# Pairs 0 and 1 of a gated-attention and MoE kernel: four tokens to a partition, running sums and v spreading on TensorE, and a new order of steps

## The chip, the cores and the metric

The kernel runs on one core of one Trainium2 chip. The metric is the device time of one execution in microseconds, the median of several runs. A core has five engines that run in parallel, each through its own list of instructions: TensorE (PE, matmuls; PEld is its weight load), VectorE (DVE), ScalarE (ACT), GpSimd (POOL) and SyncE (SP, which here only issues DMA transfers).

## The reference

```python
def _attn_ref(q, k, v, f_logit):                 # B, H, S, D = 4, 8, 768, 48
    f = 1.0 / (1.0 + np.exp(-f_logit))
    state = np.zeros((B, H, D, D))
    for t in range(S):
        state = f[:, :, t, :, None] * state + np.einsum('bhd,bhe->bhde', k[:, :, t], v[:, :, t])
        y[:, :, t] = np.einsum('bhd,bhde->bhe', q[:, :, t], state)

def _moe_ref(x, w_in, w_out):                    # x: 3072 x 384, w_in: 384 x 2048, w_out: 2048 x 384
    h = x @ w_in
    return (h * np.cos(h)) @ w_out
```

A state of 48 x 48 per batch and head decays by a gate per row and takes in one outer product of k and v per token; q reads it. The result, with the heads side by side, goes through two matmuls with h * cos(h) between them.

## The kernel before

**Pairs.** The tokens are cut into 12 pairs of 256 tokens (`PAIRS`), each for one batch and all 8 heads; three pairs in a row belong to a batch and hand on the state. A pair has two chunks of 128 tokens (`g`), and a chunk lies on 64 partitions. Partition p holds tokens 2p and 2p+1 (`e` or `x`, 0 and 1) of every head, so that a DMA moves pieces of 2 x 48 floats, 384 bytes.

**Steps of a pair n.** `f`, `k`, `q`, `v` load. `ex` and `ln` make softplus(-f), the negative logarithm of the gate, in `sp`. `fx`, `fy`, `qa`, `ka` bring the two tokens of a partition to one common point (`qa` and `ka` scale the first token of q and k). `cum` is the running sum over the 64 partitions, a matmul with a triangle of ones (`incl`); `eb` and `ei` are its exponentials with either sign, the decay (`b`) and the growth (`bi`). `qm` and `km` multiply q and k with them. `tq`, `tk` transpose the products on PE (pairs 4 to 11: by DMA), and `qkt` copies them out of PSUM. `sc` makes the scores and `am` masks them. `vb` turns v to bf16 and four `vt` copies lay it out for the next matmul. `ps` makes the outer products, `st` adds the state before, `sz` decays it. `y` (scores times v) and `yi` (q times state) share PSUM banks, and `xe` copies the result to bf16 as x.

**Halves.** Pairs 0 and 1 (`HALVES`) do the front part in two halves of four heads, 0 and 1 behind the point: `ex0.1` is pair 0, heads 4 to 7. The other pairs do it for 8 heads at once.

**MoE of unit m** (256 tokens): `h` (12 matmuls to a step j = 0 to 3, written in two parts, h1.20 and h1.21 being the parts of step 2 of unit 1), `co` the cosine on ACT (a Sin with a shift), `g` the product h * cos(h) on DVE, `o` the second matmul, `ot` the copy and `out` the store. The weights come in four slices each (`w0.j` for w_in, `w1.j` for w_out) through slots of the tile g, and `wc` turns each to bf16: h with step j needs wc0.j.

**The order** is written out by hand: the string `ORDER` lists every step with its engine (T PE, S ACT, V DVE, G POOL, Y SP) and, behind it, the numbers of the slots or PSUM banks that it writes. Each engine runs its own steps in that order; `emit` plays it, and semaphores keep the data dependences. `SLOTS` says how many buffers a tile has. A load into a slot waits until the last reader of its previous content has run, and each load on SP waits for the load eight places before it.

**Zero matmuls.** `zf0` to `zf51` multiply zeros into PSUM; their results are not used. `z...` steps fill constant parts of tiles with zeros.

## Time and profile before

| | |
|---|---|
| three runs | 182.61, 183.1, 181.85 us, median 182.61 |
| profiled execution, first to last instruction (the page gives it no other time) | span 178.2 us |
| busy: PE, DVE, ACT, POOL | 170.5, 136.6, 127.2, 112.9 us |
| matmuls and weight loads | 2475 and 2478 |
| DMA | 34.46 MB, mean 193 GB/s, 67456 of 74394 packets under 512 B |
| granted PE clock over the span | 1.00 |

The span leaves out what lies before the first and after the last instruction, so it is shorter than a run's time. A busy PE is one with a matmul in flight: matmuls overlap, and the ends in the trace are modelled. In the groups, `am<-ps,pmask` means that the instruction writes tile am from ps and pmask.

### The profile page before, as it was taken

To read this page: it belongs to the slowest core of one execution; us is meant where nothing else is said; L and a number is where in the kernel's file an instruction comes from. 1 tells how busy PE (TensorE), PEld (TensorE's weight loads), DVE (VectorE), ACT (ScalarE), POOL (GpSimd) and SP (SyncE) were. 2 spreads that over 40 slices of the span, in tenths; PEclk is the share of its full clock that TensorE was granted. 3 is DMA by queue.
4 is the path that set the end of the run, shared out by engine and by line. 5 is a ranking of instruction groups with operands and counts; after the bars stand their busy time and mean duration, and the time that the engine had idled before them with its cause. 6 is when DMAs were issued, how large, how long until landed. Compare 5 with 4: busy or idle time off the path is not lost.

```text
span 178.2 us, 5848 instructions
## 1 busy us (share of the span) xinstructions
PE 170.5 (96%) x2475; PEld 122.8 (69%) x2478; DVE 136.6 (77%) x206; ACT 127.2 (71%) x179; POOL 112.9 (63%) x145
## 2 busy tenths in 40 slices
PE   7897899999999999999999999999999999999992
PEld 2453559786668866788668886668876767777761
DVE  6479999994896989989999797983938699364640
ACT  3887597887899999888997889949754342365630
POOL 8366889797789998979978599768995000000000
PEclk9999999999999999999999999999999999999999
DMA  5999889999999999978899979995039410020042
GB/s 148 261 261 264 307 221 362 328 359 277 293 258 258 222 241 232 289 166 188 246 198 274 255 198 238 178 287 143 2 59 169 144 48 4 0 88 4 0 177 88
DMA packets 74394, 34.46 MB, mean 193 GB/s; under 512 B 67456, under 2 KB 72832, under 8 KB 74368
## 3 DMA queue, kind: packets, MB, share of 16 engines
q1 hardware_dynamic: 73408, 33.59, 78.9%
q10 hardware_dynamic: 960, 0.49, 0.9%
q8 instruction: 19, 0.31, 0.7%
q14 instruction: 7, 0.06, 0.1%
HBM read 25.17 MB, written 4.72 MB: 168 GB/s over the span
## 4 chain that ended last, share of the span: by engine, by line
PE 84%; DVE 6%; SPq 4%; DMA 3%; issue 1%; ACT 1%; DVEq 0%
PE ps L593 36%; PE ps L577 35%; PE ps L529 5%; SPq L296 4%; PE ps L455 3%; DMA k<-in_k_dram 3%; DVE am L459 2%; PE ps L477 2%; DVE qk L404 1%; PE ps L435 1%; PE ps L374 1%; DVE ps L495 1%; ACT w_in_bf L197 1%; DVE x L197 1%; PE ps L264 0%
## 5 line engine op out<-in xcount | busy, mean ns | idle before, releaser
L559 DVE TENSOR_TENSOR g<-ps,co 128x1024 bf16<-128x1024 f32 x48 | 58.0, 1222 | 20.0 <-ACT co L582 17.1
L582 ACT ACTIVATE co<-ps,halfpi 128x1024 bf16<-128x1024 f32 x48 | 53.0, 1114 | 24.5 <-PE ps L577 21.4
L593 PE MATMUL ps<-w_out_bf,g 128*128 128x384 bf16 x384 | 68.0, 326 | 0.0
L577 PE MATMUL ps<-x,w_in_bf 128*128 128x256 bf16 x576 | 66.9, 273 | 0.4 <-ACT w_in_bf L197 0.3
L577 PEld LDWEIGHTS <-w_in_bf 128*128 128x128 bf16 x576 | 55.5, 98 | 9.0 <-ACT w_in_bf L197 0.5
L593 PEld LDWEIGHTS <-g 128*128 128x128 bf16 x384 | 36.2, 98 | 21.5
L459 DVE TENSOR_TENSOR am<-ps,pmask 128x1024 bf16<-128x1024 f32 x24 | 28.8, 1219 | 4.3 <-PE ps L455 4.0
L197 POOL COPY vt<-vb 64x384 bf16<-64x384 bf16 x40 | 20.6, 516 | 3.1 <-ACT vb L197 1.3
L404 POOL TENSOR_TENSOR qk<-q,b 128x384 bf16<-128x384 f32 x21 | 20.9, 1002 | 2.0 <-DVE q L338 1.3
L404 POOL TENSOR_TENSOR qk<-k,bi 128x384 bf16<-128x384 f32 x20 | 19.9, 1001 | 0.7
L264 PE MATMUL ps<-zero 128*128 128x512 bf16 x49 | 14.8, 426 | 1.5 <-DVE zero L203 1.2
L501 DVE TENSOR_TENSOR sz<-ps,b 64x192 bf16<-64x192 f32 x40 | 14.1, 352 | 2.4 <-PE ps L477 1.6
L351 POOL TENSOR_TENSOR k<-k,f 128x384 f32<-128x384 f32 (+1 forms) x13 | 11.8, 909 | 6.0 <-DMA k<-in_k_dram 3.5
L197 ACT COPY ot<-ps 128x384 f32<-128x384 f32 (+1 forms) x15 | 6.6, 456 | 9.6 <-PE ps L593 5.0
L495 DVE TENSOR_TENSOR ps<-ps,sz 64x192 f32<-64x192 f32 x32 | 11.7, 365 | 1.8 <-PE ps L477 0.8
L329 ACT ACTIVATE f<-f 128x768 f32<-128x768 f32 (+1 forms) x14 | 10.4, 744 | 3.3 <-DMA f<-in_f_logit_dram 2.6
L363 POOL TENSOR_TENSOR sp<-ls 128x384 bf16<-128x384 f32 x10 | 10.1, 1007 | 4.0 <-ACT ls L333 3.8
L341 POOL TENSOR_TENSOR q<-f,q 128x384 f32<-128x384 f32 x10 | 10.0, 998 | 3.9 <-ACT f L344 2.8
L197 POOL CAST vb<-v 128x768 bf16<-128x768 f32 x10 | 8.6, 856 | 1.5 <-DMA v<-in_v_dram 1.5
L455 PEld LDWEIGHTS <-qkt 48*64 48x64 bf16 x384 | 6.2, 106 | 4.5 <-issue 2.4
L455 PE MATMUL ps<-qkt 48*64 48x128 bf16 x384 | 8.8, 220 | 0.5 <-DVE am L459 0.2
L264 PEld LDWEIGHTS <-zero 128*128 128x128 bf16 x52 | 4.8, 105 | 5.7 <-issue 1.9
(64 smaller groups left out, 160.9 us busy)
## 6 DMA issues: line engine op xcount, KB each, us to landing
v<-in_v_dram SPq DMA_DIRECT2D x12, 384.0 KB, 5.6
out_dram<-ot SPq DMA_DIRECT2D x22, 192.0 KB, 3.5
f<-in_f_logit_dram SPq DMA_DIRECT2D x10, 384.0 KB, 6.2
k<-in_k_dram SPq DMA_DIRECT2D x10, 384.0 KB, 6.1
q<-in_q_dram SPq DMA_DIRECT2D x10, 384.0 KB, 5.8
g<-in_moe_w_in_dram SPq DMA_DIRECT2D x4, 768.0 KB, 7.0
g<-in_moe_w_out_dram SPq DMA_DIRECT2D x4, 768.0 KB, 6.9
k<-in_k_dram SPq DMA_DIRECT2D x4, 192.0 KB, 4.7
```

Source lines behind the costliest of these rows:

```text
L197: (nc.scalar.copy if e == "ACT" else eng(e).tensor_copy)(out=o, in_=i)
L264: G.step(f"zf{i}", ("PE",), lambda e, dump=dump: nc.tensor.matmul(dump.ap, lhsT=zero[:, 0:128], rhs=zero, start=True, stop=True), writes=[ ...
L351: eng(e).tensor_mul(out=w.ap[:, :, 0, :], in0=w.ap[:, :, 0, :], in1=t.ap[:, :, 0, :])
L404: G.step(f"{nm}{n}.{u}", ("POOL", "DVE") if cut else ("POOL",), lambda e, u=u, j=j, src=src, dec=dec: eng(e).tensor_mul(out=qkp[u][j].ap[: ...
L455: nc.tensor.matmul(o[64 * h:64 * h + 64, r, 2 * a + g, :].rearrange("p (e n) -> p e n", e=2), lhsT=qkv(u)[s, 1, a, g, h, :], rhs=qkv(u)[s, ...
L459: G.step(f"am{n}.{u}", ("DVE",), lambda e, u=u, sc=sc: nc.vector.tensor_mul(out=am[u].ap.rearrange("p r b n -> p (r b) n"), in0=sc.ap.rear ...
L495: nc.vector.tensor_add(out=view()[s], in0=view()[s], in1=S0.ap[s, :, r, :])
L501: eng(e).tensor_mul(out=new.ap[s, :, r, :].rearrange("p (u a) n -> p u a n", u=2), in0=view()[s].rearrange("p (u a) n -> p u a n", u=2), i ...
L559: nc.vector.tensor_mul(out=o.rearrange("p b (n e) -> p b n e", e=2), in0=ph.ap.rearrange("p (b e n) -> p b n e", e=2, n=64), in1=co.ap.rea ...
L577: nc.tensor.matmul(ph.ap[:, i * T:(i + 1) * T].rearrange("p (g t) -> p g t", t=C), lhsT=w_in_bf[:, kk, f0:f0 + 128], rhs=xa[:, :, kk, :], ...
L582: G.step(f"co{m}.{j}", ("ACT",), lambda e, ph=ph, co=co: nc.scalar.activation(out=co.ap, in_=ph.ap, func=AF.Sin, bias=halfpi), reads=[ph], ...
L593: nc.tensor.matmul(po.ap[:, 0:DM], lhsT=gT.ap[:, j, i * C:(i + 1) * C], rhs=w_out_bf[:, j, :], start=(po.first and j == 4 * s), stop=(po.f ...
```

## The change

Pairs 0 and 1 (`QUADS`) read f, k, q and v with **four tokens to a partition**: partition 2m + a holds tokens 4m to 4m+3 of two heads of each four, the heads alternating between even and odd partitions. DMA pieces are 768 bytes. v is loaded in two halves too.

- `fx`, `qa` and `ka` of these pairs are gone. The running sum is taken for every token: `cum` runs seven wide matmuls (`every`), with triangles that connect only partitions of the same parity (`qincl`, `qstrict`), and the result is 384 wide for half a pair, not 192. `ei` is written over f, `eb` into a new tile `bq`.
- `vb` becomes two passes, each multiplying v by a column of 0 and 1 (`odd`) that keeps the heads of one parity. A new step `vs` spreads v over the partitions with 16 matmuls, and two copies from PSUM (`vt`) replace four copies from SBUF.
- `ps` multiplies pieces of 96 columns instead of 48. Masks, transposes and the gate of units 0 and 1 follow the new order of tokens.
- New constants: `cqi` (four operations on DVE), `cqs` (two) and `cqm` (seven) on POOL.
- `zf` goes from 52 to 15 steps, and the whole `ORDER` is new.

The core of the diff:

```diff
+QUADS = (0, 1)
-ZEROS = 52
+ZEROS = 15
...
         G.step(name, ("SP", "ACT") if name in ("f0.0", "f0.1") else ("SP",), lambda e: eng(e).dma_start(
-            out=val.ap.rearrange("p h e d -> p h (e d)"),
-            in_=tok.rearrange("h (p e) d -> p h (e d)", e=2)), writes=[val])
+            out=val.ap.rearrange("p (r f) e d -> p r (f e d)", f=2) if quad else val.ap.rearrange("p h e d -> p h (e d)"),
+            in_=tok.rearrange("h (m t) d -> m h (t d)", t=4) if quad else
+            tok.rearrange("h (p e) d -> p h (e d)", e=2)), writes=[val])
...
+        sp, bt, bi = Val(spS), Val(bqS if quad else bS), f if quad else Val(biS)
...
+            if quad:
+                continue
             G.step(f"fx{n}{u}", ("ACT",), lambda e, t=t, s=s: gate_of(e, t, s), reads=[s], writes=[te], table="E")
...
+        def every(e, u):
+            w, o = sph[u].ap, pcs[u].ap[:, 0:DM].rearrange("p (j r d) -> p j r d", j=4, r=2)
+            for j in range(4):
+                row = w[:, j, None, :, 0:D]
+                nc.tensor.matmul(o[:, j:4], lhsT=qincl, rhs=row.broadcast_to([128, 4 - j, 2, D]), start=(j == 0), stop=False)
+                if j:
+                    nc.tensor.matmul(o[:, 0:j], lhsT=qstrict, rhs=row.broadcast_to([128, j, 2, D]), start=False, stop=False)
+            for j in range(4):
+                nc.tensor.matmul(pcs[u].ap[:, DM:DM + 4], lhsT=w[:, j].rearrange("p r d -> p (r d)"),
+                                 rhs=qhalf.rearrange("p a g -> p (a g)"), start=False, stop=(j == 3))
...
+                def only(e, a=a):
+                    o, i = vb.ap[:, a].rearrange("p j h d -> p h j d"), byj(vv.ap)
+                    if e == "ACT":
+                        nc.scalar.activation(out=o, in_=i, func=AF.Copy, scale=odd[:, a:a + 1])
+                    else:
+                        eng(e).tensor_scalar_mul(out=o, in0=i, scalar1=odd[:, a:a + 1])
+                G.step(f"vb{n}.{a}", ("POOL", "ACT"), only, reads=[vv, qi_v], writes=[vbp[a]])
...
+            def spread(e):
+                for a in range(2):
+                    for j in range(4):
+                        for g in range(2):
+                            t = slice(64 * g, 64 * g + 64)
+                            rows = pv.ap.rearrange("p (g x) -> p g x", g=2)[32 * j:32 * j + 32, g, 0:DM]
+                            nc.tensor.matmul(rows.rearrange("p (u a n) -> p a u n", u=2, a=2)[:, a], lhsT=qsel[t, a, :],
+                                             rhs=vb.ap[t, a, j].rearrange("p (u r) d -> p u (r d)", u=2),
+                                             start=(a == 0), stop=(a == 1))
+            G.step(f"vs{n}", ("PE",), spread, reads=[vb, qs_v], writes=[pv])
```

**On SP**, the load queue from its first entry. Names carry the slot number: f_0 is slot 0 of f. Shapes of 128x4x96 and 128x2x192 are halves of a pair (0.197 MB). Before, f0.1 stands first, then f1.1, k0.1, the whole v0, q0.1, k0.0 (f0.0 goes over ACT's queue):

```order
L296 DMA f_0_94<-in_f_logit_dram 128x4x96
L296 DMA f_1_95<-in_f_logit_dram 128x4x96
L296 DMA k_0_97<-in_k_dram 128x4x96
L296 DMA v_2_105<-in_v_dram 128x8x96
L296 DMA q_0_100<-in_q_dram 128x4x96
```

Now f0.1, f1.0, k0.1, both halves of v0, k0.0, f1.1, q0.1 and k1.0 come first, then q0.0, k1.1 and both q1. The second piece shows what follows on them: f3, f2 (into the slot of f0), v1, the first two slices of w_in, q3 (into the slot of q0) and k3:

```order
L329 DMA f_1_101<-in_f_logit_dram 128x2x192
L329 DMA f_0_100<-in_f_logit_dram 128x2x192
L329 DMA k_2_105<-in_k_dram 128x2x192
L329 DMA v_0_109<-in_v_dram 128x2x192 x2
L329 DMA k_2_105<-in_k_dram 128x2x192
```

```order
L329 DMA q_1_107<-in_q_dram 128x2x192 x2
L329 DMA f_2_102<-in_f_logit_dram 128x8x96
L329 DMA f_1_101<-in_f_logit_dram 128x8x96
L329 DMA v_1_110<-in_v_dram 128x2x192 x2
L313 DMA g_2_155<-in_moe_w_in_dram 128x3x512
L313 DMA g_4_157<-in_moe_w_in_dram 128x3x512
L329 DMA q_0_106<-in_q_dram 128x8x96
L329 DMA k_0_103<-in_k_dram 128x8x96
```

v0 has moved ahead of q, and f2, which now waits for the last reader of f0, stands ahead of v1 and of the first weights.

**On DVE**, from its first product (km0.1, the first row of each piece) on. Before, the scaling of q (L338) and of k (L351) and products (L404) alternate with the state (L501, L495):

```order
L404 TENSOR_TENSOR qk_118<-k_97,bi_116 128x8x48
L231 MEMSET vt_124 128x16x2x8
L338 SCALAR_TENSOR_TENSOR q_100<-f_94,q_100 128x4x48
L404 TENSOR_TENSOR qk_118<-q_100,b_113 128x8x48
L404 TENSOR_TENSOR qk_118<-k_97,bi_116 128x8x48
L197 COPY qkt_127<-ps_159 128x1024
L231 MEMSET qk_119 128x32x8
L501 TENSOR_TENSOR sz_136<-ps_159,b_113 64x4x48
```

Now there are three products (L459), and the state and the first masked scores (L558) follow:

```order
L459 TENSOR_TENSOR qk_123<-k_105,f_101 128x2x4x48
L260 MEMSET sz_146 128x192
L459 TENSOR_TENSOR qk_123<-k_105,f_101 128x2x4x48
L459 TENSOR_TENSOR qk_123<-q_106,bq_132 128x2x4x48
L609 TENSOR_TENSOR sz_147<-ps_171,bq_132 64x4x48 x2
L603 TENSOR_TENSOR ps_168<-ps_168,sz_147 64x192
L609 TENSOR_TENSOR sz_146<-ps_168,bq_132 64x4x48
L194 COPY qkt_136<-ps_169 128x1024
L558 TENSOR_TENSOR am_141<-ps_171,qmask 128x1024
```

The other five products of the two pairs have moved to **POOL**, whose list from the selection of v0 (L480) to the cast of the first weights reads now:

```order
L480 TENSOR_SCALAR vq_129<-v_109,odd 128x4x4x48 x2
L260 MEMSET vt_135 128x16x2x16
L459 TENSOR_TENSOR qk_123<-q_106,bq_132 128x2x4x48
L459 TENSOR_TENSOR qk_124<-k_104,f_100 128x2x4x48
L459 TENSOR_TENSOR qk_124<-q_107,bq_131 128x2x4x48 x2
L459 TENSOR_TENSOR qk_124<-k_104,f_100 128x2x4x48
L403 TENSOR_TENSOR sp_114<-ls_116 128x8x48
L480 TENSOR_SCALAR vq_130<-v_110,odd 128x4x4x48
L403 TENSOR_TENSOR sp_112<-ls_115 128x8x48
L194 CAST w_in_bf<-g_155 128x3x512
```

and read, from the cast of v0 to the same place, before (L351 scales k, L363 adds the two tokens' sums):

```order
L197 CAST vb_121<-v_105 128x768
L351 TENSOR_TENSOR k_97<-k_97,f_94 128x4x48
L197 COPY vt_124<-vb_121 64x8x48
L231 MEMSET sz_136 128x384
L197 COPY vt_124<-vb_121 64x8x48 x2
L363 TENSOR_TENSOR sp_106<-ls_110 128x8x48
L197 CAST vb_120<-v_104 128x768
L197 COPY vt_123<-vb_120 64x8x48
L404 TENSOR_TENSOR qk_117<-q_101,b_111 128x8x48
L197 COPY vt_123<-vb_120 64x8x48
L351 TENSOR_TENSOR k_99<-k_99,f_95 128x4x48
L363 TENSOR_TENSOR sp_107<-ls_109 128x8x48
```

The copies of v have left POOL, and four products more stand between v and the first weight cast.

293 lines of the change are left out of this document (181 added, 112 removed).

## The prediction

> **What bounds the kernel now.** I read the share of busy time first, then three stretches of the span, then the timeline around the place where they meet.
>
> ```profile
> PE 170.5 (96%) x2475; PEld 122.8 (69%) x2478; DVE 136.6 (77%) x206; ACT 127.2 (71%) x179; POOL 112.9 (63%) x145
> ...
> 0.00:25.19 25.19, 21.20 (x287) 11.06 (x291) 19.27 (x48) 17.91 (x38) 17.51 (x31) 1.00 1.00 241
> 25.19:32.85 7.66, 7.27 (x128) 6.00 (x129) 7.38 (x12) 6.52 (x8) 7.09 (x7) 1.00 1.06 341
> 32.85:174.97 142.12, 142.02 (x2060) 105.69 (x2060) 109.62 (x147) 102.49 (x134) 88.34 (x108) 1.00 0.77 180
> ...
> L264 PE MATMUL ps<-zero 128*128 128x512 bf16 x49 | 14.8, 426 | 1.5 <-DVE zero L203 1.2 <-issue 0.2
> ```
>
> The stretch rows give start and end, length, then busy time of PE, PEld, DVE, ACT and POOL, the granted clock, DMA share and GB/s. From 32.85 us to the last matmul PE is busy 142.02 of 142.12 us: nothing that shortens another engine's work there can shorten the span. Before 25.19 PE looks busy too, but 14.8 us of it is the zero matmuls (their recorded ends overlap), which compute nothing. So the kernel is a **front**, in which PE waits for data, and a **block** of 142.1 us of PE work. The block begins with the third weight slice, h1.20:
>
> ```profile
> 21.85 2.87 POOL L197 CAST w_in_bf<-g 128x1536 bf16<-128x1536 f32 x2
> 25.19 1.47 PE L577 MATMUL ps<-x,w_in_bf 128*128 128x256 bf16 x12
> 31.34 1.46 ACT L197 CAST w_in_bf<-g 128x1536 bf16<-128x1536 f32 x1
> 32.85 4.10 PE L577 MATMUL ps<-x,w_in_bf 128*128 128x256 bf16 x36 [0.30 <-ACT w_in_bf L197]
> ```
>
> Both orders place the same PE steps ahead of h1.20, except that sc3.1 now follows it. **The question is when h1.20 can start.**
>
> **Loads.** Tensors arrive in the order of SP's queue.
>
> ```profile
> 4.00:14.00 10.00, 9.46 (x111) 5.05 (x110) 6.17 (x19) 8.37 (x21) 5.36 (x10) 1.00 1.27 261
> 28.00:30.00 2.00, 2.00 (x20) 1.79 (x19) 1.96 (x4) 1.17 (x2) 1.92 (x3) 1.00 1.03 390
> 7.45 0.82 POOL L197 CAST vb<-v 128x768 bf16<-128x768 f32 x1 [0.80 <-DMA v<-in_v_dram]
> 9.06 0.65 POOL L351 TENSOR_TENSOR k<-k,f 128x192 f32<-128x192 f32 x1 [0.79 <-DMA k<-in_k_dram]
> 9.68 0.52 ACT L329 ACTIVATE f<-f 128x384 f32<-128x384 f32 x1 [1.17 <-DMA f<-in_f_logit_dram]
> ```
>
> From 4 to 14 us the engines move only 384-byte pieces, at 261 GB/s; from 28 to 30 the 2048-byte pieces of the weights, at 390. Half a tensor (0.197 MB) takes 0.75 us at 261. The three waits fit 2.95 us plus 0.75 per half: v0 completes the sixth half (7.45), k0.0 is the eighth (8.95, seen 9.06), f1.0 the ninth (9.70, seen 9.68). After the change the sixteen halves come in 768-byte pieces, which this trace does not show at the front; the bounds are 0.75 (no gain) and 0.50 (the rate of 2048 bytes). A straight line through the time per piece and engine at both sizes (384 B at 261/16 GB/s, 23.5 ns; 2048 B at 390/16, 84 ns) gives 37.5 ns, hence 0.60 us a half. I take 0.60. Then v0 is there at 6.55, q0.0 (eleventh) at 9.55, q1.1 (fourteenth) at 11.35, f3 and f2 (1.5 each at 261) at 12.85 and 14.35, v1 at 15.55. Weight slices at 0.786 MB take 2.1 each: w0.0 17.65, w0.1 19.75; after q3 and k3, w0.2 lands at **24.9** (27.3 at 0.75, 23.3 at 0.50).
>
> The Trainium skill ("DMA: Bandwidth & Descriptors", Specifications) puts the smallest transfer that runs at line rate at 512 B, with smaller ones read, modified and written. By it 768-byte halves would run like the weights, which is the 0.50 bound; the two rates above agree in direction, by a factor of 1.5. With it q0.0 and w0.2 land at 8.45 and 23.3, h1.20 would be set by DVE and ACT (below), and the sum would end 0.3 us lower.
>
> f2 now waits for km0.0 on DVE, because its slot holds f0, into which the growth factors are written; q3 waits for POOL's q0 product. Behind f2 on SP stand v1, w0.0, w0.1 and q3. The data ahead of f2 keep the queue busy until about 11.9 (f3 is complete at 12.85); ei0.0, ninth on ACT's list at 0.5 us each from 3.9, ends near 8.4 and km0.0 near 9. So I cost both waits at nothing. A km0.0 later than about 10.8 would delay everything behind f2 one for one.
>
> **DVE.** From its first product to the end of the second gate:
>
> ```profile
> 10.00:20.00 10.00, 8.28 (x156) 4.47 (x156) 9.16 (x17) 8.89 (x20) 6.84 (x11) 1.00 1.16 284
> 20.00:30.00 10.00, 9.37 (x180) 6.84 (x182) 9.33 (x17) 7.16 (x11) 9.05 (x9) 1.00 0.89 281
> 6.68 0.56 DVE L404 TENSOR_TENSOR qk<-k,bi 128x384 bf16<-128x384 f32 x1 [1.79 <-POOL k L351]
> 29.13 2.36 DVE L559 TENSOR_TENSOR g<-ps,co 128x1024 bf16<-128x1024 f32 x2
> L404 DVE TENSOR_TENSOR qk<-k,bi 128x384 bf16<-128x384 f32 x4 | 3.0, 754 | 2.3 <-POOL k L351 2.3
> L404 DVE TENSOR_TENSOR qk<-q,b 128x384 bf16<-128x384 f32 x3 | 2.7, 912 | 0.2
> L338 DVE SCALAR_TENSOR_TENSOR q<-f,q 128x192 f32<-128x192 f32 x4 | 1.5, 383 | 0.7 <-DMA q<-in_q_dram 0.7
> L351 DVE TENSOR_TENSOR k<-k,f 128x192 f32<-128x192 f32 x1 | 0.4, 359 | 0.0
> L197 DVE CAST x<-ps 128x384 bf16<-128x384 f32 x2 | 1.1, 553 | 0.1
> ```
>
> That is 6.68 to 31.49, with DVE busy over 9 of every 10 us from 10 on. Gone are the leading products, 1.5 + 0.4, and four of seven decay products: 5.7 becomes three at the mean of 0.75, or 2.3. A spread copy (vt1.0) of the size of the x copies adds 0.55. The sum is -1.9 - 3.4 + 0.55 = -4.75. The new constants (cqi, four small operations) come before the first product and in the time that it waited anyway, so the start stays at 6.8 (the end of ei0.1, sixth on ACT's list). The second gate ends at 31.49 - 4.75 + 0.1 = **26.9**. If the three products cost 0.56 or 1.35 each (the extremes beside an idle and a busy POOL), it is 26.3 or 28.7.
>
> **ACT** must finish the cast of w0.2 before h1.20.
>
> ```profile
> L333 ACT ACTIVATE sp<-f 128x384 bf16<-128x384 f32 x4 | 2.0, 518 | 0.1
> L333 ACT ACTIVATE ls<-f 128x768 f32<-128x768 f32 x2 | 1.7, 832 | 0.0
> L347 ACT ACTIVATE f<-sp 128x192 f32<-128x192 bf16 x4 | 1.4, 359 | 0.1
> L395 ACT ACTIVATE b<-ps 128x392 f32<-128x392 f32 x2 | 1.0, 500 | 0.0
> L395 ACT ACTIVATE bi<-ps 128x384 f32<-128x384 f32 x2 | 1.0, 490 | 0.0
> L197 ACT COPY qkt<-ps 128x1024 bf16<-128x1024 bf16 x2 | 2.0, 1012 | 2.9 <-PE ps L435 2.9
> L582 ACT ACTIVATE co<-ps,halfpi 128x1024 bf16<-128x1024 f32 x4 | 4.5, 1115 | 1.1 <-PE ps L577 1.0
> L582 ACT ACT_TABLE_LOAD x1 | 1.3, 1283 | 0.0
> ```
>
> New list: eight Exp and Ln at 0.52 (4.1); eight decays, now 384 wide, at 0.5 (4.0); one qkt 1.0; three vt at 0.5 (1.5); for pairs 2 and 3 four passes at 0.83, four at 0.53 and four decays (3.3 + 2.1 + 2.0); one selected v 0.83; x 0.48; table 1.28; two cosines 2.2; the cast 1.46. Together 24.2. The groups of this view, eight of them shown, sum to about 27 before, where the stretch rows count 24.4 busy, because neighbours overlap; a tenth off leaves 21.8. With 1 us of waits and a start at 3.9 (the first half is there by 3.55 to 3.7) the cast ends at **26.7**; with no overlap, 29.1.
>
> **POOL** feeds it and casts w0.0 for the first h.
>
> ```profile
> L404 POOL TENSOR_TENSOR qk<-q,b 128x384 bf16<-128x384 f32 x3 | 3.0, 1030 | 1.4 <-DVE q L338 1.3
> L363 POOL TENSOR_TENSOR sp<-ls 128x384 bf16<-128x384 f32 x2 | 2.1, 1037 | 1.5 <-ACT ls L333 1.5
> L197 POOL COPY vt<-vb 64x384 bf16<-64x384 bf16 x6 | 3.6, 603 | 0.2
> ```
>
> Six spread copies go; four more products come, and three passes that multiply v by a 0/1 column, each d long. From q0.0 at 9.55: five products at 1.0, two adds at 1.04, one d and the cast at 1.46 end at 18.1 + d. The row nearest to d is the v cast (0.82, same size, one input); as two products it would be 2.0. With 0.86 the first weights are ready at 19.0 and **h0.00 starts near 19.5** against 25.19. From there the same nine steps as before, which took 7.66 us, end at 27.2.
>
> **PE** itself gets dearer and is covered. Each running sum streams 1536 columns instead of 384: at 0.236 us per 512 (second row under the rivals) 0.7 instead of 0.2 us, 2 us for four; two spreads of 16 matmuls cost 0.3 to 1.3 each. All stand where 37 zero matmuls (37 x 0.236 = 8.7 us) are taken out. Without that cover they would cost 4 us.
>
> **The sum.** The latest of the four is 27.2; I allow 0.2 for handing over: h1.20 at 27.4 instead of 32.85, -5.45. sc3.1 has moved into the block: +0.35. The block had 0.1 us of waits; for an order that no trace shows I add 0.5. Span 178.2 - 4.6 = 173.6. The profiled execution has no time of its own beside its span; the three runs lie 3.7 to 4.9 us above it, the median 4.4, so 173.6 + 4.4 = **178.0 us**. The bounds of the loads, products and overlap put h1.20 between 26 and 29.3, 176.6 to 179.9.
>
> **Rivals.** A difference under 1% (1.8 us) is what a measurement here hardly tells from none.
>
> *The clock falls back.*
>
> ```profile
> 1.19 4.02 PE L264 MATMUL ps<-zero 128*128 128x512 bf16 x9 [1.19 <-DVE zero L203]
> 7.79 1.89 PE L264 MATMUL ps<-zero 128*128 128x512 bf16 x8
> 14.00:16.00 2.00, 1.30 (x13) 0.63 (x12) 1.90 (x4) 1.03 (x3) 1.94 (x3) 1.00 1.16 273
> L459 DVE TENSOR_TENSOR am<-ps,pmask 128x1024 bf16<-128x1024 f32 x4 | 4.9, 1222 | 0.1
> ```
>
> The first nine zero matmuls take 447 ns each, later ones 236: PE starts at half speed, and the zeros keep it busy afterwards. In the new order PE has little to do between sc0.0 and sc1.0: sc1.0 waits for qkt1.0, which stands on DVE behind two am of 1.22 us, so that some 3.5 us hold sixteen transposes and four zeros, about 1.8 us of work. If that drops the clock, the 3 us of scores and y ahead of h0.00 double, and the first h steps run at half rate until it rises: 1.7 to 4 us lost, 179.7 to 182. Against it: 14 to 16 us is nearly as thin now (1.30 of 2 us, zeros included) and the row shows 1.00. The Trainium skill ("TensorE: Matmul & The Clock Gate", Part 1) has the clock halved after an idle window of about 3.4 us and restored after a busy one; by it the removal of zeros is the risk of this change, though no gap here reaches 3.4 us. Chance 0.14.
>
> *The gain is given back at pairs 2 and 3.*
>
> ```profile
> 44.37 0.83 ACT L197 CAST vb<-v 128x768 bf16<-128x768 f32 x1 [0.43 <-DMA v<-in_v_dram]
> 51.21 1.51 PE ps L529 x100
> ```
>
> v2 is just in time now: ACT waits for it. Behind w0.2 stand five weight slices and q2, k2, f4, v3, v2 (10.5 + 7.5 us): v2 at 42.9, only 1.5 earlier, where PE wants y2 5 us earlier. Of the 6.8 us between cast and y2, copies need about 3. So the wait is 0 to 3 us: 178.5 to 181. Chance 0.17.
>
> *POOL becomes the bound, and it is slower.* If the v selection is dear, the first cast ends at 15.6 + 3d once d exceeds 1.2. At d = 2.0 that is 21.6, costing 2 us (180); at 3.2 nothing is won; at 3.8 it is 184.5. For it: no row shows this form. Against: the cast row. Chance 0.08.
>
> *More is won*: 390 GB/s and cheap products, h1.20 at 25.5, 176. Chance 0.06. The forecast keeps 0.55.
>
> **Range and chances.** 175.6 to 182.0 takes in the forecast with its bounds, the larger gain, and the first two rivals; POOL's and the tails stay out. Half of the clock rival and 0.6 of the second lie below 180.8: faster 0.78, same 0.13, slower 0.09.
>
> **What would show it.** Right: h0.00 near 19.5, h1.20 near 27.4, PE solid from there; GB/s near 330 from 4 to 11 us; three DVE products near 0.75; granted clock 1.00. Wrong: a v selection over 1.2 us, a clock of 0.5 between 12 and 24 us, PE waiting for vt or y2 at 43 to 48, or a solid block longer than 143 us.

## The result and the profile after

The changed kernel is slower: 189.18 us median (188.72 to 190.18) against 182.86 in the same session; ratio 1.0375, 95% interval 1.0324 to 1.0426. Forecast were 178.0 us and a range up to 182.0. All ratios below are to the kernel before, timed on the same chip. Ratios and intervals leave out slow runs, those more than 1.5% above the fastest of their kernel; the times in us are medians of all runs.

From the page of the kernel after: PE's share of busy time, the granted clock in 40 slices of 4.67 us, and the engines of the chain that ended last.

```profile
PE 170.8 (91%) x2491; PEld 123.8 (66%) x2493; DVE 140.2 (75%) x207; ACT 136.0 (73%) x187; POOL 109.7 (59%) x137
PEclk9996999987999999999999999999999999999999
PE 67%; DVE 18%; POOL 5%; issue 5%; DMA 2%; ACT 2%; DVEq 0%; POOLq 0%
```

PE is as busy as before (170.8 against 170.5 us) in a longer span, the clock has two dips, and DVE's share of the chain has trebled (6% before). Its stretches, cut at h0.00 and h1.20 (columns as in the prediction):

```profile
0.00:25.71 25.71, 17.37 (x304) 11.23 (x306) 15.66 (x42) 17.11 (x33) 19.79 (x33) 0.93 0.90 275
25.71:34.17 8.46, 7.04 (x112) 5.84 (x113) 7.67 (x13) 8.03 (x9) 8.38 (x9) 1.00 0.87 272
34.17:183.56 149.39, 146.38 (x2079) 106.75 (x2076) 116.49 (x152) 110.58 (x145) 81.51 (x97) 0.99 0.67 166
```

h0.00 starts at 25.71 instead of the forecast 19.5, h1.20 at 34.17 instead of 27.4 (most of that delay is there at h0.00 already), and the block takes 149.4 us instead of 143.0 (142.1 + 0.35 + 0.5). This execution took 188.72 us, 1.8 above its span, where the forecast added 4.4. The forecast of 178.0, plus 6.8 at h1.20, 6.4 in the block and 0.1 behind the last matmul, less 2.6 around the span, is the measured 188.7.

What PE waited for, from its timeline (start, length; in brackets the idle time before and what ended it), with POOL's and DVE's rows at the same places, and two groups of instructions:

```profile
12.54 0.36 PE L575 MATMUL ps<-vq,qk 64*64 64x96 bf16 x16 [3.71 <-POOL vq L480]
33.73 0.61 PE L534 MATMUL ps<-ident,qk 128*128 128x128 bf16 x8 [1.38 <-DVE g L667]
38.74 0.42 PE L554 MATMUL ps<-qkt 48*64 48x128 bf16 x16 [0.99 <-DVE g L667]
40.55 2.45 PE L685 MATMUL ps<-x,w_in_bf 128*128 128x256 bf16 x12 [0.63 <-DVE g L667]
8.10 4.39 POOL L480 TENSOR_SCALAR vq<-v,odd 128x768 bf16<-128x768 f32 x2 [2.63 <-DVE qk L459]
24.18 2.88 POOL L194 CAST w_in_bf<-g 128x1536 bf16<-128x1536 f32 x2
29.94 3.74 DVE L667 TENSOR_TENSOR g<-ps,co 128x1024 bf16<-128x1024 f32 x2
34.98 7.33 DVE L667 TENSOR_TENSOR g<-ps,co 128x1024 bf16<-128x1024 f32 x4
L480 POOL TENSOR_SCALAR vq<-v,odd 128x768 bf16<-128x768 f32 x3 | 6.6, 2203 | 2.6 <-DVE qk L459 2.6
L478 ACT ACTIVATE vq<-v,odd 128x768 bf16<-128x768 f32 x1 | 0.9, 920 | 0.0
L667 DVE TENSOR_TENSOR g<-ps,co 128x1024 bf16<-128x1024 f32 x48 | 63.0, 1336 | 16.4 <-ACT co L690 15.9
```

Two dear instructions stand out. A selection of v takes POOL 2.20 us (forecast 0.86), and ACT 0.92. And a gate of units 0 and 1, which now brings four interleaved groups of tokens into order, takes 1.85 us (3.74 for two) where 1.22 was the price of all gates before: 5 us more of DVE where PE waits for DVE.

### The profile page after: what moved, and what is told of

Its sections match the earlier page's. It is cut to its first block, busy times and chain, and to the rows that moved or that the text cites. A ratio compares the mean times of both kernels' runs of the same rounds, so it can differ in the third digit from the quotient of the medians.

```text
span 186.9 us, 5878 instructions
## 1 busy us (share of the span) xinstructions
PE 170.8 (91%) x2491; PEld 123.8 (66%) x2493; DVE 140.2 (75%) x207; ACT 136.0 (73%) x187; POOL 109.7 (59%) x137
## 4 chain that ended last, share of the span: by engine, by line
PE 67%; DVE 18%; POOL 5%; issue 5%; DMA 2%; ACT 2%; DVEq 0%; POOLq 0%
PE ps L685 29%; PE ps L701 27%; DVE g L667 6%; PE ps L637 4%; DVE am L558 3%; POOL vq L480 3%; DVE ps L603 3%; DVE sz L609 3%; PE ps L554 2%; POOL qk L459 2%; DVE ot L194 2%; DMA f<-in_f_logit_dram 2%; PE ps L585 2%; PE ps L534 1%; DVE x L194 1%
## 5 line engine op out<-in xcount | busy, mean ns | idle before, releaser
L667 DVE TENSOR_TENSOR g<-ps,co 128x1024 bf16<-128x1024 f32 x48 | 63.0, 1336 | 16.4 <-ACT co L690 15.9
L685 PE MATMUL ps<-x,w_in_bf 128*128 128x256 bf16 x576 | 69.2, 275 | 2.1 <-DVE g L667 0.9
L558 DVE TENSOR_TENSOR am<-ps,pmask 128x1024 bf16<-128x1024 f32 x20 | 23.8, 1220 | 2.6 <-PE ps L554 2.2
L467 POOL TENSOR_TENSOR qk<-q,b 128x384 bf16<-128x384 f32 x20 | 19.8, 1000 | 1.9 <-issue 1.4
L194 POOL COPY vt<-vb 64x384 bf16<-64x384 bf16 x25 | 12.4, 501 | 10.1 <-ACT vb L194 8.0
L194 DVE COPY ot<-ps 128x384 f32<-128x384 f32 (+1 forms) x15 | 7.8, 527 | 8.2 <-PE ps L701 4.0
L194 ACT COPY ot<-ps 128x384 f32<-128x384 f32 (+1 forms) x11 | 4.9, 446 | 11.3 <-PE ps L701 11.2
L609 DVE TENSOR_TENSOR sz<-ps,b 64x192 bf16<-64x192 f32 x32 | 11.2, 353 | 1.0 <-PE ps L585 0.3
L389 POOL TENSOR_TENSOR k<-k,f 128x384 f32<-128x384 f32 x10 | 10.0, 998 | 0.2
L371 ACT ACTIVATE ls<-f 128x768 f32<-128x768 f32 x10 | 8.4, 844 | 0.3
```

The lines of the kernel that those rows point to most:

```text
L194: (nc.scalar.copy if e == "ACT" else eng(e).tensor_copy)(out=o, in_=i)
L467: G.step(f"{nm}{n}.{u}", ("POOL", "DVE") if cut else ("POOL",), lambda e, u=u, j=j, src=src, dec=dec: eng(e).tensor_mul(out=qkp[u][j].ap[: ...
L558: G.step(f"am{n}.{u}", ("DVE",), lambda e, u=u, sc=sc: nc.vector.tensor_mul(out=am[u].ap.rearrange("p r b n -> p (r b) n"), in0=sc.ap.rear ...
L609: eng(e).tensor_mul(out=new.ap[s, :, r, :].rearrange("p (u a) n -> p u a n", u=2), in0=view()[s].rearrange("p (u a) n -> p u a n", u=2), i ...
L667: nc.vector.tensor_mul(out=o.rearrange("p b (n e) -> p b n e", e=E), in0=ph.ap.rearrange("p (b e n) -> p b n e", e=E, n=C // E), in1=co.ap ...
L685: nc.tensor.matmul(ph.ap[:, i * T:(i + 1) * T].rearrange("p (g t) -> p g t", t=C), lhsT=w_in_bf[:, kk, f0:f0 + 128], rhs=xa[:, :, kk, :], ...
```

## The experiments

### The gate

**before_gate4** puts only the new gate into the kernel before.

```diff
-    gate(gv, ph, co, T)                            # e=2, n=64
+    gate(gv, ph, co, T, 4 if n < 2 else 2)         # e=E, n=C // E
```

> The kernel before, with the gates of units 0 and 1 interleaving four token groups instead of two, and nothing else; this leaves the tokens of these units in another order than the output wants, so it only prices the gate. Theory G: the eight gates go from 1.22 to about 1.85 us, DVE has 5 us more between 29 and 45 us, where it is busy nine tenths of the time; PE waits for g, and the time rises by 2.5 to 4.5 us, to 185.4 to 187.4. Rival F: DVE's idle stretches take it up, under 1 us: below 183.9. The difference between this and the whole loss of 6.3 us is what the front and the new order lose.

185.54 us, ratio 1.018 (1.0121 to 1.0238): 2.2 to 4.3 us for eight gates. Its DVE and PE timelines:

```profile
29.11 3.72 DVE L559 TENSOR_TENSOR g<-ps,co 128x1024 bf16<-128x1024 f32 x2
31.06 1.47 PE L577 MATMUL ps<-x,w_in_bf 128*128 128x256 bf16 x12 [0.35 <-DVE g L559]
40.04 1.47 PE L577 MATMUL ps<-x,w_in_bf 128*128 128x256 bf16 x12 [1.19 <-DVE g L559]
46.05 1.47 PE L593 MATMUL ps<-w_out_bf,g 128*128 128x384 bf16 x8 [0.68 <-DVE g L559]
```

The gates cost 1.86 us there too, and PE waits where it did not wait before. Theory G holds.

**gate_order** keeps the kernel after, but walks the groups in the outer loop: reads straight, the write at a stride.

```diff
-    out=o.rearrange("p b (n e) -> p b n e", e=E),      # in0, in1: "p (b e n) -> p b n e"
+    out=o.rearrange("p b (n e) -> p b e n", e=E),      # in0, in1: "p (b e n) -> p b e n"
```

> The kernel after, with the gate's three operands walked in another order: the four interleaved token groups become the outer loop, so that PSUM and the cosine are read straight through and the 2-byte result is written at a stride of four. Theory G (the gate): in the trace of after the eight gates of units 0 and 1 take 1.83 to 1.87 us where the other forty take 1.22, which is 5 us more of DVE between 29.9 and 47 us; the PE waits for g there (1.38, 0.99 and 0.63 us) and the clock of 0.50 from 40.86 to 44.27 (1.7 us lost) hang on it. Then the eight gates fall to 1.2 to 1.3 us, the waits shrink to under 0.5 together, the clock stays 1.00 there, and the time falls by 3 to 5 us, to 184 to 186. Rival F (the front): the loss is made ahead of the first h step, at 25.7 us; the gates get cheaper, but weights casts or ACT set the same steps, and the time stays within 1 us of 189.2. Rival W: a stride on the write costs what a stride on the read costs; the eight gates stay above 1.7 us and nothing changes.

193.84 us, ratio 1.0658 (1.0616 to 1.0699). Rival W, and worse than W: two gates of units 0 and 1 take 4.77 us, and the mean over all 48 is 1.51.

```profile
31.04 4.77 DVE L667 TENSOR_TENSOR g<-ps,co 128x1024 bf16<-128x1024 f32 x2
L667 DVE TENSOR_TENSOR g<-ps,co 128x1024 bf16<-128x1024 f32 x48 | 70.3, 1506 | 14.4 <-ACT co L690 13.9
```

**rows** takes the reordering off DVE: straight gates, and the store puts the rows right.

```diff
-    gate(gv, ph, co, T, 4 if n in QUADS else 2)
+    gate(gv, ph, co, T, 1 if n in QUADS else 2)
...
+    if n in QUADS: dst = dst.rearrange("(p e) d -> e p d", e=4)
```

> The kernel after, with the gates of units 0 and 1 walking everything straight through, and the token order put right by the store instead: each of the four stores of pairs 0 and 1 writes its 128 rows to every fourth row of the output, in the same pieces of a row. Priced so far: with the reads at a stride the eight gates take 1.85 us, with the writes at a stride of four 2.5 us, and the strided reads alone made the kernel before 3.7 us slower. Theory G (the gate): the eight gates fall to about 1.22, DVE has 5 us less between 30 and 47, PE's waits for g and the clock of 0.50 from 40.86 to 44.27 go, and the time falls by 3.3 to 4.5 us, that is to 1.013 to 1.02 of the kernel before. Rival A: ACT's cosines and casts become the bound of the same steps; under 2 us is won, 1.027 or more. Under both the front stays as it is: h0.00 near 25.7.

187.61 us, ratio 1.0355 (1.028 to 1.043): not to be told from the kernel after. Yet the gates did what was asked (shortest, median, longest of 48), and PE reached its long run of h steps at 55.60 instead of 59.93 us:

```profile
L667 DVE TENSOR_TENSOR g<-ps,co x48: 1204/1225/1226, 30.6 to 174.5; 128x1024 bf16<-128x1024 f32 x48
55.60 9.34 PE L685 MATMUL ps<-x,w_in_bf 128*128 128x256 bf16 x84 [0.38 <-DVE x L194]
69.62 0.64 PE L554 MATMUL ps<-qkt 48*64 48x128 bf16 x32 [1.72 <-DMA qkt<-qk]
103.27 0.52 PE L637 MATMUL ps<-qkt,sz 128*32 128x128 bf16 x24 [1.22 <-DVE sz L609]
```

4.3 us won, although h0.00 started 0.7 us later (26.42) behind two stretches of 3.4 us at half clock instead of one; and waits of 1.72, 0.34 and 1.22 us met behind it. The first is for the transposes of pair 4, a place that the prediction never looked at. Theory G was right on the gate and wrong on the end.

### The selection of v

**select_act** moves two of POOL's three selections to ACT (S behind the point is ACT, G POOL).

```diff
-vb0.1:G0 ei0.0:S vb0.0:G ps0.1:T7,1
+vb0.1:G0 ei0.0:S vb0.0:S ps0.1:T7,1
-vb1.0:S1 fx2:S ad3:G2 fx3:S vb1.1:G
+vb1.0:S1 vb1.1:S fx2:S ad3:G2 fx3:S
```

> The kernel after, with two of the three selections of v that POOL does moved to ACT (vb0.0 and vb1.1; ACT already does vb1.0 in 0.92 us, POOL takes 2.20). Theory S (the selection): PE's wait of 3.71 us that ends at 12.54 is POOL's pair of selections, 8.10 to 12.49; with one on each engine it ends near 10.4, the clock stays 1.00 from 13.5 to 17, and the second pair's selection no longer stands between POOL's two additions ahead of the first weight cast. The first h step starts 3 to 4 us earlier (21.7 to 22.7 instead of 25.71) and the time falls to 185 to 187. Rival G (the gate): the front gains as much, but the third weight slice's h step waits for the gates of 1.85 us, so that less than 1.5 us reaches the end: 187.7 to 189. Rival N: ACT, given 1.8 us more, becomes late for eb0.1 and the decays, and h0.00 gains under 1 us.

187.37 us, ratio 1.0213 (1.0127 to 1.0299). POOL's and PE's timelines:

```profile
7.88 2.55 POOL L480 TENSOR_SCALAR vq<-v,odd 128x768 bf16<-128x768 f32 x1 [2.41 <-DMA v<-in_v_dram]
23.16 1.49 PE L685 MATMUL ps<-x,w_in_bf 128*128 128x256 bf16 x12 [0.48 <-ACT b L448]
31.21 0.61 PE L534 MATMUL ps<-ident,qk 128*128 128x128 bf16 x8 [1.37 <-DVE g L667]
```

h0.00 is 2.55 us earlier, less than the 3 to 4 of theory S, and the clock stays at 1.00, so this is POOL's time and the clock's together; the time gains about 1.6% of 182 us, 3 us at the middle of wide intervals. The gates' waits are still all there.

### The clock

**zeros_vs0** and **zeros_ps0** add fourteen zero matmuls to the kernel after: behind ps0.1, the step that waits for v, and ahead of it.

```diff
-km1.0:G1 vs0:T4
+km1.0:G1 zf15:T4 ... zf28:T4 vs0:T4           # zeros_vs0
-vb0.0:G ps0.1:T7,1
+vb0.0:G zf15:T4 ... zf28:T4 ps0.1:T7,1        # zeros_ps0
```

> The kernel after, with fourteen zero matmuls put into PE's wait ahead of the spreading of v (8.8 to 12.5 us; 14 x 0.24 = 3.3 us). Theory C (the clock): the clock is 0.50 from 13.55 to 16.97 because PE was busy only 1.01 us of the 3.41 before; filled, it stays 1.00, PE's 3.4 us of work there take 1.7, the first h step comes 1 to 1.7 us earlier and the time falls to 187.5 to 188.2. Rival P: POOL, which works from 8.1 to 16 without a break, sets the front; PE finishes earlier and waits longer, h0.00 moves under 0.5 us and the time stays within 0.5 of 189.2. The clock from 40.86 to 44.27 should not change by either.

191.58 us, ratio 1.0532 (1.0486 to 1.0578): neither theory was tested, since PE runs its list in order and the zeros came after the wait. The clock still fell, from 12.8 to 16.2. They delayed h0.00 by 3.5 us, to 29.24, and the end by about 2.9: a delay in the front goes through.

> The kernel after, with fourteen zero matmuls ahead of ps0.1, the step that waits 3.7 us for the selected v. (With the same fourteen behind that step they cost 3.5 us of PE time at the half clock, since PE runs its list in order.) Theory C (the clock): 8.9 to 12.3 us is now busy, the clock stays 1.00 from 13.5 to 17, the work there takes half the time, and the first h step comes 0.5 to 1.7 us earlier; time 187.3 to 188.5 if the kernel before is at 182.5. Rival P: POOL and ACT set the front; under 0.4 us of h0.00 and of the time.

187.25 us, ratio 1.0314 (1.0256 to 1.0372). The clock is 1.00 throughout. PE's step behind the selection and h0.00, and POOL's wait for ACT's decay, first here and then in the kernel after:

```profile
13.48 0.36 PE L575 MATMUL ps<-vq,qk 64*64 64x96 bf16 x16 [1.69 <-POOL vq L480]
25.21 1.48 PE L685 MATMUL ps<-x,w_in_bf 128*128 128x256 bf16 x12 [0.56 <-ACT b L448]
17.22 1.00 POOL L459 TENSOR_TENSOR qk<-q,bq 128x384 bf16<-128x384 f32 x1 [0.44 <-ACT bq L444]
17.73 1.00 POOL L459 TENSOR_TENSOR qk<-q,bq 128x384 bf16<-128x384 f32 x1 [1.90 <-ACT bq L444]
```

h0.00 starts 0.50 us earlier, at the lower end of theory C and beyond rival P's 0.4. But v0 came late in this execution: POOL began its selections at 9.05 instead of 8.10. From the step behind them to h0.00 it took 11.73 us instead of 13.17 (12.54 to 25.71), and the 1.4 us are what POOL waited less for ACT. So the half clock did cost the front about 1.4 us here (one execution of each kernel); what the end gains lies within the intervals. The second dip is gone too, but the block is only 0.7 us shorter (148.7), because PE waits 0.9 us longer for gates.

**before_zeros15** takes 37 zero matmuls out of the kernel before (zf15 to zf51 out of `ORDER`, `ZEROS = 15`).

> The kernel before without 37 of its 52 zero matmuls (the first fifteen stay), nothing else changed. The prediction counted the 37 as cover: 8.7 us of PE time that later work could take. Theory C: with them gone PE idles for over half of some 3.4 us between 8 and 24, the clock falls to 0.50 once or twice, and 1 to 3 us are lost. Rival N: PE waits for the other engines there anyway, and the time stays within 1% of the kernel before, with a lower clock or without.

182.51 us, ratio 1.0064 (1.0023 to 1.0105). Its stretches of 10 us show 0.65 and then half speed:

```profile
10.00:20.00 10.00, 5.40 (x137) 4.40 (x137) 8.92 (x17) 8.61 (x19) 6.37 (x10) 0.65 1.19 293
20.00:30.00 10.00, 8.62 (x162) 6.00 (x154) 7.34 (x13) 6.55 (x11) 9.01 (x9) 0.50 0.86 274
```

The clock is 0.50 from 13.1 to 30.2. The first h step takes 2.74 us instead of 1.47, and h1.20 starts at 35.36, 2.5 us later than in the kernel before:

```profile
25.68 2.74 PE L577 MATMUL ps<-x,w_in_bf 128*128 128x256 bf16 x12
35.36 4.11 PE L577 MATMUL ps<-x,w_in_bf 128*128 128x256 bf16 x36 [0.40 <-ACT w_in_bf L197]
```

So the front does pay for the clock, within the 1.7 to 4 us that the prediction's rival gave it. The runs show only 1.2 us of it (0.4 to 1.9): the block of this execution took 142.7 us, with 0.2 us of waits. Theory C (1 to 3 us) and rival N (within 1%) both fit.

### Both, and the loads

**rows_select** joins straight gates and select_act; **rows_one** leaves vb1.1 on POOL; **rows_queues** is rows_select with the two halves of v0 issued by ACT.

```diff
-vb0.1:G0 ei0.0:S vb0.0:G                      # rows_one: rows, and
+vb0.1:G0 ei0.0:S vb0.0:S
-k0.1:Y2 v0.0:Y0 ... cum0.1:T6 v0.1:Y          # rows_queues: rows_select, and
+f0.0:S1 v0.1:S0 v0.0:S ... k0.1:Y2 ... cum0.1:T6
```

> Both edits together: straight gates with the order put right by the store, and the two selections of v moved from POOL to ACT. If the gate (3.3 to 4.5 us) and the selection (1.2 to 2.6 us so far) are separate losses, they add: 0.995 to 1.007 of the kernel before, h0.00 near 23.2, h1.20 near 30.3 against 32.85 in the kernel before. Rival A: with the gates cheap and ACT given 1.8 us more, ACT (91 to 100% busy from 10 to 30 us) sets the h steps; the two do not add, and it is 1.01 or more. If, beyond these two, nothing had been wrong with the prediction, the time would be 4 us below the kernel before, 0.978; what is missing then lies ahead of h0.00, predicted at 19.5.

185.74 us, ratio 1.0211 (1.0133 to 1.029): the same as select_act alone, so the two do not add in the time. h0.00 starts at 22.35, h1.20 at 30.01, 2.8 us earlier than in the kernel before. POOL, ACT and PE:

```profile
20.38 1.46 POOL L194 CAST w_in_bf<-g 128x1536 bf16<-128x1536 f32 x1 [0.62 <-DMA g<-in_moe_w_in_dram]
28.15 1.47 ACT L194 CAST w_in_bf<-g 128x1536 bf16<-128x1536 f32 x1 [0.28 <-DMA g<-in_moe_w_in_dram]
66.72 0.64 PE L554 MATMUL ps<-qkt 48*64 48x128 bf16 x32 [2.31 <-DMA qkt<-qk]
```

Now w0.0 (20.4, forecast 17.65) and w0.2 (28.1, forecast 24.9) are waited for themselves.

> The kernel after with straight gates (order put right by the store) and only vb0.0 moved from POOL to ACT; vb1.1 stays on POOL. With both moved, ACT was busy 9 to 10 of 10 us from 10 to 30 and POOL stood idle 2.6 us ahead of its first weight cast; there w0.0 landed at 20.4, w0.1 at 22.6 and w0.2 at 28.1 (by POOL's and ACT's waits for them), the last against 24.9 in the prediction. Theory D (the loads): with the gate and the selection cheap, the landings of the weight slices set h0.00 (22.4) and h1.20 (30.0 = landing of w0.2, 28.1, plus a cast of 1.46 and its place on ACT); 0.9 us less on ACT changes h1.20 by under 0.4 us and the time by under 0.5 against the kernel with both moved (1.021 of before). Theory A (ACT): ACT sets them; h1.20 and the time fall by 0.7 to 1 us.

185.43 us, ratio 1.0122 (1.0026 to 1.0217); h1.20 at 29.80. ACT had a selection less and h1.20 moved 0.2: theory D on that point. The times cannot be told apart.

> As the kernel with straight gates and both selections on ACT, and the two halves of v0 issued by ACT, which is idle until its first Exp at 4.3, instead of by SP. In the trace of after SP takes 0.61 to 0.66 us to issue one half of a tensor in 768-byte pieces, eighteen in a row, and the DMA engines are only 0.70 busy from 0 to 10 us: the loads go at the pace of the issue, where the prediction counted 0.60 a half by the bytes. Theory I (the issue): every load behind v0 comes 1.0 to 1.3 us earlier (q0.0 at 10.4 instead of 11.5, w0.0 at 19.3 instead of 20.4), v0 at 6.5 to 7 instead of 7.85, and the first h step and h1.20 0.8 to 1.3 us earlier; time 1.012 to 1.016 of before. Rival: the DMA engines catch up by 16 us anyway (their share is 1.0 from 8 us on); w0.0 moves under 0.4 us and the time under 0.5.

184.97 us, ratio 1.0189 (1.013 to 1.0249). w0.0 arrives at 20.1 instead of 20.4, and v0 later, not earlier (POOL waits for it until 8.34 instead of 7.85): the rival. The pace of issue at the start is not what makes w0.0 late.

### The block behind h1.20

**rows_one_tq** and **best1** put the transposes of pairs 4 and 5 ahead of the loads f7, v5 and v6 on SP (best1 with v0 on ACT and eight zeros more).

```diff
-f7:Y2 ... tq4.0:Y3 v5:Y1 ... v6:Y0 ... tq5.1:Y2 km5.0:G tq5.0:Y1
+tq4.0:Y3 ... tq5.1:Y2 km5.0:G tq5.0:Y1 v5:Y1 f7:Y2 v6:Y0
```

> As the kernel with straight gates and vb0.0 on ACT, and on SP the four transposing DMAs of pairs 4 and 5 go ahead of the loads f7, v5 and v6 instead of between them. With both selections moved PE waited 2.31 us at 66.7 for a transposed qkt of pair 4, which SP had taken 3.6 us to issue, while the DMA engines were busy from 30 to 66 us (share 1.00 to 1.06 of the span there, in the block as a whole 0.73). Theory Q (the queue): the gain of the front is given back there, not at pairs 2 and 3; with the transposes ahead the wait goes and the time falls by 1.5 to 2.5 us. Rival B (bandwidth): the loads that go behind are missed instead (v5, v6, f7 a little later), or the transposes wait for POOL's products; under 0.7 us.

191.78 us, ratio 1.0486 (1.038 to 1.0592): rival B. PE's wait for sc4.0 falls to 0.67 us from 1.61, and a load put behind the transposes is missed at once: SP takes 7.9 us to issue three transposes, f7 goes out at 67 us instead of 55, and ACT waits 6.76 us for it, then PE for ACT:

```profile
74.23 1.04 PE L637 MATMUL ps<-am,vt 128*32 128x128 bf16 x32 [4.71 <-ACT vt L194]
```

> All edits so far: straight gates, vb0.0 on ACT, v0's halves issued by ACT, the transposes of pairs 4 and 5 ahead of three loads, and eight zero matmuls in PE's waits ahead of ps0.1 and vs1 to hold the clock (single runs of the kernels with both selections moved showed granted clocks of 0.98 to 0.99 and were up to 2 us longer than those at 1.00). If the losses add, the time is 1.021 - 0.010 (transposes) - 0.006 (issue) - 0.005 (clock) = 1.000 of before, between 0.993 and 1.01. What would still be missing against the prediction: about 1 us of loads and 2.7 us by which PE is busy longer in the block than in the kernel before.

188.09 us, ratio 1.0359 (1.0255 to 1.0463), spoilt by the same move (2.11 us for vt at 72.8).

**before_again** is a second profile of the kernel before.

> The kernel before, once more, for a second profiled execution. The sum of the prediction was made against one execution with a span of 178.2 us and added 4.4 us to it, the distance to the runs. All later runs lie 1.8 us above their own spans, so the execution shown was itself a quick one (180.0). Theory V: executions of one kernel differ in the block too; here h1.20 starts within 0.5 us of 32.85 and the block is 143 to 145 us long, with waits or PE time that the first profile does not show. Rival: the difference lies ahead of h1.20, and the block is again 142.1.

182.56 us. Its last stretch, and the one large wait in it:

```profile
32.93:177.54 144.61, 142.80 (x2060) 105.71 (x2060) 109.65 (x147) 102.38 (x134) 87.81 (x107) 1.00 0.76 175
140.18 0.42 PE L455 MATMUL ps<-qkt 48*64 48x128 bf16 x16 [1.40 <-DMA qkt<-qk]
```

Theory V: h1.20 at 32.93 as before, but a block of 144.6. The 142.1 was one quick execution.

**rows_shift** moves o5.3 and o4.3 ahead of sc4.0 and pair 7's state steps ahead of ot7; **best2** adds v0 on ACT and five zeros ahead of ps0.1.

```diff
-sc4.0:T4 ... sc4.1:T6 ... o5.3:T am4.0:V0 o4.3:T
+o5.3:T o4.3:T sc4.0:T4 ... sc4.1:T6 ... am4.0:V0
-ot7:V0 ... st7.10:V sz7.10:V1 ... st7.11:V sz7.11:V
+st7.10:V sz7.10:V1 st7.11:V sz7.11:V ot7:V0
```

> As the kernel with straight gates and vb0.0 on ACT, with two moves in the order: PE does o5.3 and o4.3 (1.3 us of matmuls whose data are there) ahead of sc4.0, which waited 1.6 to 2.3 us for transposes at 66; and DVE does the state steps of pair 7 ahead of ot7, which waited 1.3 us for a store while PE waited 1.2 us for those state steps at 99. Theory W (waits in the block): they are part of what the block has beyond 142.1 + 0.35; 1.5 to 2.3 us go, the block from h1.20 on is near 146, the runs in which the clock fell (0.987 to 0.991) become rarer because PE no longer idles over half of 3.4 us at 64 to 67; time 1.000 to 1.006 of before. Rival B: the loads and transposes there are late by the same amount for the next steps (y4), and under 0.7 us goes.

184.09 us, ratio 1.0119 (1.0076 to 1.0162), as rows_one: rival B, with a block of 148.1 instead of 146. The two waits shrink (1.6 to 0.5 at 67, 1.2 to nothing at 99), and two of 0.4 appear for transposes at 93.

> The same, with v0's halves issued by ACT and five zero matmuls ahead of ps0.1. If the earlier loads add the 0.3 to 0.6 us that h1.20 gained from them before, and the zeros hold the clock, 0.996 to 1.003 of before; if not, as the kernel without these two.

183.12 us, ratio 1.0071 (1.0044 to 1.0098): the whole interval lies above the expected 0.996 to 1.003. h1.20 at 29.48:

```profile
29.48:177.29 147.81, 144.76 (x2080) 105.95 (x2076) 112.47 (x152) 111.97 (x147) 83.58 (x99) 1.00 0.71 173
```

**hybrid** and **after_block** run best2 and the kernel after in their own order up to h1.20 and behind it in the order of the kernel before, with free buffers chosen anew; **hybrid2** mends a bad choice of the first.

> The last kernel's steps (straight gates with the order put right by the store, vb0.0 on ACT, v0 issued by ACT, five zero matmuls ahead of ps0.1) in that kernel's order up to h1.20, and from there on in the order of the kernel before; the steps are the same, a dozen buffer numbers differ. In all kernels with the new order so far the block from h1.20 to the last matmul took 147.8 to 150.0 us, wherever it began (29.4 to 34.2) and with dear or cheap gates; in two executions of the kernel before it took 142.1 and 144.6. Theory O (the order): the extra length is the new order's own, its PE time (144.8 against 142 to 143) and its waits; with the old order behind h1.20 the block is 142.5 to 145, h1.20 starts near 29.5 to 30, and the time is 0.975 to 0.99 of before, faster than both kernels. Rival D (supply): loads and POOL cannot deliver pairs 2 to 5 any earlier than they do now, so a front that ends 3 us earlier meets new waits; the block is 146 or more and the time 0.992 or more.

188.07 us, ratio 1.0264 (1.0189 to 1.034), with the stall that hybrid2's expectation describes.

> The kernel after, unchanged up to h1.20 (selection on POOL, interleaved gates), and from there on the steps in the order of the kernel before. Theory O: the block falls from 149.4 to 144 to 147 (142 to 145, and 1 to 3 us of waits for the eight dear gates, which cost the kernel before 3.7 us); h1.20 stays near 34 and the time is 1.015 to 1.028 of before instead of 1.0375. Rival D: as the front is no earlier than before, supply is no limit here; if the block still takes 149, its length comes from the gates and not from the order.

189.23 us, ratio 1.0335 (1.027 to 1.04), not to be told from the kernel after. The block is 147.3, with 3.7 us of waits, 2.4 of them for g. But the old order has sc3.1 ahead of h1.20, which starts at 35.64, and the last matmul ends only 0.6 us earlier than in the kernel after (182.95 against 183.56). Neither theory O nor rival D is shown.

> As the kernel with the mended front and the old order behind h1.20, with two things put right that the joining itself had made: the staging buffers of the weight slices are taken longest-free first (SP had stood 11.9 us at 26 us before it could issue the second half of w1, because its buffer still held w1.2; PE then waited 1.03 and 2.80 us for w_out and ran at half clock), and three memsets of buffers go to DVE's idle time at 5 us, with sc3.1 behind h1.21. Theory O (the order): without these stalls the block is 143 to 145.5 us, h1.20 near 29.5 and the time 0.98 to 0.993 of before. Rival D (supply): PE meets other waits for loads or for DVE and POOL between 36 and 52 us; the block is 146.5 or more and the time 0.998 or more.

183.4 us, ratio 1.0103 (1.0021 to 1.0185): rival D. PE, POOL, and the stretch from 30 to 40 us:

```profile
31.98 2.78 PE L685 MATMUL ps<-x,w_in_bf 128*128 128x256 bf16 x24 [1.06 <-DVE g L667]
38.28 2.76 PE L701 MATMUL ps<-w_out_bf,g 128*128 128x384 bf16 x16 [1.21 <-POOL w_out_bf L194]
44.65 0.42 PE L554 MATMUL ps<-qkt 48*64 48x128 bf16 x16 [1.33 <-DVE am L558]
36.76 1.46 POOL L194 CAST w_out_bf<-g 128x1536 bf16<-128x1536 f32 x1 [3.12 <-DMA g<-in_moe_w_out_dram]
30.00:40.00 10.00, 7.56 (x81) 5.95 (x79) 8.61 (x8) 6.25 (x6) 6.81 (x7) 1.00 1.09 333
```

PE is 3.75 us ahead of the kernel before at h1.20 (29.10 against 32.85) and only 0.5 at the first o step (38.28 against 38.77). It waits because POOL waits 3.1 us for a slice of w_out, while the DMA engines are at a share of 1.09. PE is busy for 143.6 us of this block. No version here beats the kernel before.

The main kernels in one table (times in us, read from PE's timelines; waits are those of 0.15 us and more behind h1.20):

| kernel | h1.20 | block | waits | ratio |
|---|---|---|---|---|
| before, two executions | 32.85, 32.93 | 142.1, 144.6 | 0, 1.6 | 1 |
| before_gate4 | 33.84 | 145.7 | 2.4 | 1.018 |
| after | 34.17 | 149.4 | 2.7 | 1.0375 |
| rows | 33.50 | 149.0 | 4.5 | 1.0355 |
| select_act | 31.65 | 150.0 | 4.6 | 1.0213 |
| rows_select | 30.01 | 149.2 | 4.4 | 1.0211 |
| rows_one | 29.80 | 148.0 | 3.7 | 1.0122 |
| best2 | 29.48 | 147.8 | 2.9 | 1.0071 |
| hybrid2 (old order behind) | 29.10 | 148.7 | 4.9 | 1.0103 |

## Why the prediction was wrong, step by step

**POOL (first term that failed).** "The row nearest to d is the v cast (0.82)", so the sum took 0.86: measured 2.20. The rival "POOL becomes the bound" named this and got a chance of 0.08. Its formula, 15.6 + 3d, gives 22.2 for the first cast's end; it was 25.6. The formula let POOL run alone, but PE stood 3.71 us behind the first two selections, ACT behind PE, and POOL then waited 1.90 us for ACT's decay; 1.4 us of this chain hang on the half clock (zeros_ps0). v0 itself came at about 7.9 (POOL waits for it until 7.85 to 7.93 in select_act, rows and rows_select) and not at 6.55. With two selections off POOL, and the clock at 1.00, h1.20 came 2.5 us earlier.

The Trainium skill ("GPSIMD Engine Reference", 4.1 Engine selection) has one-input operations on POOL run at roughly line rate. For the cast the trace agrees (0.82 us, where ACT takes 0.83); for the multiplication by a column over the same 128 x 768 it does not (2.20, where ACT takes 0.92). Both read v in another order than it lies in, in runs of 48; no run here separates the multiplication from its order of access.

**The gate (a term that was missing).** The diff showed E = 4, and the sum let the gates stay at 1.22. 0.63 us for each of eight, on the engine that the prediction itself found nine tenths busy. Alone in the kernel before it cost 1.8%. In the new order straight gates brought h1.20 1.6 us forward (select_act to rows_select) and the end no measurable gain.

**Loads.** "GB/s near 330 from 4 to 11 us": measured 272, or 0.72 us a half; from 10 to 20 us it was 335. SP took 0.61 to 0.66 us to issue each half (SP's timeline, two halves of q):

```profile
8.36 1.27 SPq L329 DMA_DIRECT2D q<-in_q_dram  x2
```

With the front mended, w0.2 came at 28.1 instead of 24.9: the largest part of what kept h1.20 at 29.5 to 30 instead of 27.4. The pace of issue explains little of it, by rows_queues. There 5.6 MB had been moved when w0.0 arrived, though the queue holds only 4.7 MB up to it: loads behind it had moved along, where the sum let each finish in turn. What share of the delay that is, no run shows.

**DVE** was right in its own work up to the gates (three products of 0.56, 0.56 and 1.24 us) and PE's longest wait for it ahead of h0.00 was 1.19 us (am, at 18.90). **ACT**: in rows_select the cast of w0.2 ended at 29.6, 2.9 later than forecast, after a wait for the load.

**The solid block.** "142.1 + 0.35 + 0.5" took for a constant what was one quick execution with every wait at zero. Two executions of the same kernel differ by 2.5 us there. Of the 4.8 us that the block of the kernel after has beyond the second one (149.4 - 144.6), by the stretch rows 1.2 are idle time (3.0 against 1.8) and 3.6 PE time (146.4 against 142.8): half of the 3.4 us at half clock from 40.86, which is 1.7, and 1.9 more, 0.35 of it sc3.1. Without the dip these 1.7 us are not all won: zeros_ps0 gave 0.9 of them back in waits for gates.

**Around the span** 4.4 us were added and 1.8 measured, in every later run: by that the profiled execution was 2.6 us quicker than the median, and the difference was taken for something outside the span.

**Rivals.** The clock did fall to 0.50 (13.55 to 16.97), which the sum left out with a chance of 0.14; it cost the front about 1.4 us (zeros_ps0), near the rival's lower end of 1.7. "The gain is given back" was right in kind: every kernel that brought h1.20 forward by 3 us found waits of 3 to 5 us behind it. The place was wrong: not v2 at pairs 2 and 3, but w_out at 38 (hybrid2) or the transposes of pair 4 at 66 (rows_select), where loads fill the DMA engines.

**Open.** hybrid2 shows for the old order that an earlier front meets a full DMA queue and late gates. For the new order it is not shown what of its 148 us is supply and what its own. Its PE time at full clock is 144.3 to 144.8 us; the same steps in the old order take 143.6 (hybrid2, with sc3.1), and the kernel before 142.0 and 142.8. So about 1 us of PE time comes with the new order; why is not shown.
